# Loading k of two chunks at once, splitting the first-stage table, and rewriting VectorE's order in the first pass

## The chip, the cores and the metric

The kernel runs on one core of a Trainium2 chip. Its engines work side by side, each through its own queue in order: TensorE (PE, matmuls and transposes into PSUM; PEld is its weight load), VectorE (DVE), ScalarE (ACT), GpSimd (POOL) and SyncE (SP), which issues nearly all transfers (DMAs). Engines wait for one another by semaphores. The metric is device time in microseconds (us), lower is better: the median of 3 runs before is 234.06 (233.75 to 234.32).

## The reference

Two branches share one normalized input, and their results are added to it. Sequence length S is 2048, width D is 640, hidden width F is 1728; all tensors are bf16.

```
x  = A_q;  xn = (x - mean) / sqrt(var + 1e-5)          # per row, over D
# branch A: a shift convolution of 4 taps, a product, a long convolution
k_shift[s] = sum over t of k[s - t] * shift_k[:, t]    # t = 0..3, zero before the start
kv  = k_shift * v
y   = irfft(rfft(kv padded to 2S) * rfft(ssm_k padded to 2S))[:S]
y   = y + kv * ssm_D
A   = xn * y
# branch B: a gated unit
h   = sigmoid(xn @ w_gate) * (xn @ w_up)
B   = h @ w_down
out = x + A + B
```

## The kernel before

Rows are laid out 16 to a partition: row 16 p + b is on partition p, block b (b = 0..15). The 640 columns are 5 chunks c of 128.

**The gated unit** runs in four passes t, one per group of 4 blocks (512 rows). A pass needs the 4 blocks of xn transposed (xnT): in the first pass TensorE transposes them, in the others SyncE issues four transposing DMAs (xn_turn, L250). Then for each of 13 slices of 128 hidden columns come a gate product (gate_mm), its sigmoid on ScalarE (gate_ev), an up product (up_mm), and VectorE's product of the two into hT (up_ev, L286). A last slice, both_mm, holds the remaining 64 columns of both. Then the down products: for each block bb and each half of the columns, 7 + 7 matmuls (down_mm, part 0 and part 1, L315), after which VectorE adds the PSUM result to x (down_ev, L320). The PSUM pool of these products has 4 buffers, so a product waits until the fourth one before it has been read.

**Normalization** of groups 1 to 3: VectorE makes the statistics of 4 blocks (ln_norms, L200 and L204), GpSimd the factor (ln_pow, L212, once for the group), and VectorE normalizes (ln_xn, L217); for group 1, ScalarE does blocks 2 and 3 (ln_xn_act, L229), with a shift from GpSimd.

**The long convolution** is a Fourier transform in two stages, by chunk. For chunk c, VectorE makes kv in 16 steps (kv_op): per half of 8 blocks one product acc = k * tap 0 (L348), three products with later taps (L352), each added to acc (L354), and the product with v (L357). k lies in a tile kx with 3 extra rows ahead, the halo, from the partition before. There were two such tiles, one for even and one for odd chunks. The taps come by a broadcast load into sraw and are reordered into sc (taps: chunk 0 on GpSimd, others on ScalarE). The filter ssm_k is loaded to hn and transposed by VectorE in two steps (h_turn, L334) into the same tile kvh as kv; D is added to its first element on GpSimd (add_D, L328). Then stage one is eight steps per chunk (st1_mm: half h of the table and 4 blocks each, L374 and L376), copied out (st1_ev) and written to a buffer in DRAM (wr1). Stage two, the product in the frequency domain and the way back follow, through DRAM again.

**The order** of everything is written out by hand: each letter of the string ORDER takes the next step of one chain (m: first loads, g: products of the gated unit, u: VectorE's part of them, k: kv_op, H: h_turn, l: normalization, e: xn_turn, a and A: stage one and its copies, and so on). Each engine runs its instructions in that order. The tables and loads are issued by SyncE in the order of the list of chain m. Many transfers are under way at once; SyncE waits with an issue when the buffer it fills is still read, when an earlier transfer that shares its semaphore hasn't landed, or when the queue takes no more.

Of the kernel before, what the change touches and what calls it, by code (L numbers as in the profile page):

```python
# [34 lines left out]
def _tables():  # L35

    p = np.arange(P)  # L40
    k1 = p + 0.25
    s1 = np.zeros((P, NB, 2, P))
    for b in range(NB):
        psi = 2 * np.pi * k1[None, :] * (16 * p + b)[:, None] / 2048.0
        s1[:, b, 0, :] = np.cos(psi)
        s1[:, b, 1, :] = -np.sin(psi)
    tb = s1.transpose(3, 2, 1, 0) / 2048.0
# [10 lines left out]
def kernel(  # L58
# [14 lines left out]
    nc = tc.nc  # L73
# [24 lines left out]
    S1t = res.tile([P, NB, 2, P], U16, name="S1t")  # L98
    TBt = res.tile([P, 2, NB, P], U16, name="TBt")
    SMt = res.tile([P, 3, 32], U16, name="SMt")  # L100
    S1 = S1t.bitcast(BF16)
    TB = TBt.bitcast(BF16)
    SM = SMt.bitcast(BF16)
# [31 lines left out]
    def load_h(c):  # L135

        d = cin[c]
        d["hn"] = cv.tile([P, 4, 512], BF16, name="hn")
        d["dr"] = cv.tile([1, P], BF16, name="dr")
        sync.dma_start(d["dr"][:, :], Drow[:, c * P:(c + 1) * P])  # L140
        for q in range(4):
            src = A_ssm_k[c * P:(c + 1) * P, 512 * q:512 * q + 512].rearrange("(k r) t -> r k t", k=4)
            sync.dma_start(d["hn"][32 * q:32 * q + 32, :, :], src)

    def load_taps(c):
        cin[c]["sraw"] = cv.tile([P, 4 * P], BF16, name="sraw")
# [178 lines left out]

    def add_D(c):
        h0 = cin[c]["kvh"][0:1, 1, 0:2, :].rearrange("p b c -> p (b c)").rearrange("p (c e) -> p e c", e=2)[:, 0, :]
        nc.gpsimd.tensor_tensor(h0, h0, cin[c]["dr"][:, :], ALU.add)  # L328

    def h_turn(c, n):  # L330

# [34 lines left out]
    def st1_mm(c, n):  # L366

        h, n4 = divmod(n, 4)
        if n == 0:
            chunks[c]["d1"] = dr.tile([P, 2, NB, 2 * P], BF16, name="d1", bufs=2)  # L370
        pss[n] = ps = psC.tile([P, 4, 2 * P], F32, name="ps1", tag="c")
        for i in range(4):
            b = 4 * n4 + i
            nc.tensor.matmul(ps[:, i, 0:P], lhsT=S1[:, b, h, :], rhs=cin[c]["kvh"][:, 0, b, :], start=True, stop=True)  # L374
            hp = cin[c]["kvh"][:, 1, :, :].rearrange("p b c -> p (b c)").rearrange("p (b c e) -> p b e c", b=8, e=2)
            nc.tensor.matmul(ps[:, i, P:2 * P], lhsT=S1[:, b, h, :], rhs=hp[:, b // 2, b % 2, :], start=True, stop=True)  # L376

    def st1_ev(c, n, copy=act_copy):
        d = chunks[c]
# [19 lines left out]
    def rd2(s):  # L399

        c, s4 = divmod(s, 4)
        at = spare.get(s)
        if at is None:
            t2 = cv.tile([P, 8, 2 * P], BF16, name="t2", bufs=2)[:, :, :]
        else:
            t2 = (xn[:, 12:NB, :].rearrange("p b d -> p (b d)")[:, 0:2048] if at == 2 else
                  S1[:, 8 * at:8 * at + 8, :, :].rearrange("p b h k -> p (b h k)")).rearrange("p (r e) -> p r e", r=8)
# [43 lines left out]
    def inv1_ev(y, n, copy=act_copy):  # L451
        d = chunks[y // 2]
        if n == 0:
            d["ao", y] = kxs[1][:, 0:NB, :] if y >= 7 and y % 2 else cv.tile([P, 16, P], BF16, name="ao")[:, :, :]
# [14 lines left out]
    def rdb(c, n):  # L469

        d = chunks[c]
        if c >= 3 and n == 1:
            bi = kxs[0][:, 0:NB, :].rearrange("p (h b) c -> p h b c", h=2)
        elif c and n == 1:
            bi = S1[:, 8:NB, :, :].rearrange("p (h b) s c -> p h (b s) c", h=2)
        else:
            bi = cv.tile([P, 2, 8, P], BF16, name="bi")[:, :, :, :]
        src = d["d2"].rearrange("r (q h b) c -> (r q) h (b c)", q=NQ, h=2)
        sync.dma_start(bi.rearrange("p h b c -> p h (b c)"), src[:, :, 1024 * n:1024 * n + 1024])
        d["bi", n] = bi  # L480
# [8 lines left out]
                                 start=(h == 0), stop=(h == 1))  # L489

    def inv2_q(c, m):
        chunks[c]["yx", m] = yx = cv.tile([P, 4, P], BF16, name="yx")
# [58 lines left out]
    for t in range(4):  # L551
        for fc in range(0 if t else 2, 13):
            step("g", gate_mm, t, fc)
            step("s", gate_ev, t, fc)
            step("g", up_mm, t, fc)
            step("u", up_ev, t, fc)
        step("g", both_mm, t)
        step("s", both_ev, t)
        step("u", both_mul, t)
        firsts = [(0, 0, 0), (0, 1, 0), (0, 0, 1), (0, 1, 1)]  # L560
        for bb, e, part in firsts + [(k // 2, k % 2, n) for k in range(2, 8) for n in range(2)]:
            step("g", down_mm, t, bb, e, part)
            if part:
                step("u", down_ev, t, bb, e)
# [4 lines left out]
    def ks(c):  # L569
        return [(load_halo, c), (load_k, c, 0, 8), (load_k, c, 8, NB)]  # L570

    def vs(c):
        return [(load_v, c, 0, 8), (load_v, c, 8, NB)]

    for k in ((load_w, sync, 512, 1024, 0),
              (load_w, sync, 512, 1024, 1),
              (load_taps, 0),
              (sync.dma_start, SMt[:], SMd.ap()),
              (load_w, sync, 1024, 1280, 0),
              (load_w, sync, 1024, 1280, 1),  # L580
              (load_wd, sync, 0, 7),
              *ks(0),
              (load_w, sync, 1280, FF, 0),
              (load_w, sync, 1280, FF, 1),
              *hs(0),
              *vs(0),
              (load_wd, sync, 7, NFC),
              (sync.dma_start, S1t[:], S1d.ap()),
              *hs(1),
              (load_x, sync, 1),  # L590
              *ks(1),
              *vs(1)):
        step("m", *k)
    for k in ((load_x, sync, 2), (load_x, sync, 3), (sync.dma_start, TBt[:], TBd.ap())):
# [62 lines left out]
    step("o", store, NB - 1, NB, 4 * P, DM)  # L657

    ORDER = """
    mmggmmsgmuggmsgmgsuZumgggssumkgkguskugkkmsgugmmmmgkgmksgmuggHskkHkgsmukkgDumsgggkusumgTmkgkukagaumHg  # L660
    lllAKlgAatkwuAmmmakPPlAkgalAkkTwgaggagkegeugAxxDkkaeAaAgeKwaugkuAHkuggkAukkwsgkgkkgnustagukKKgghakA
    sulrwAsakggluglsaksAugHggkAVrubkkkBlswKBukgggaTVsgpkusukawgDkHPlngAaAaskgAKwAkukgskpbgtkBsllBugauAk
    gagpsAaguswVpakAguhkHHAgrgDkwcgVklguCkkraeCagAgkAbuBkuBkkggKgkbBKpggBaeualwukkggeIuurlTklAehrgwtVbBB
    ggagkAagppswuAagkuaKswrgpAAkaHAskWgHupDgakuVsAggswucglJukkgkrCsbgpBugaBaAgAWkkgsbspugPkrBgwpgsRnFku
    kgprcwgCJusgbgusgpuBdBWppbqrgsdBlRuqgBcqlCggJbsggksuBupgllkBbBgrqkWBgeaaeAAuppwdgaduRegaIAgrugpaAqae
    qggupAwcCqpJguugdbgFBgbBqqgugBppdcpWCuJqgrpsgqbgBsuwFgrgqsbuBgpBRsuWgpdcpqqdguJgqCsrrbFBgsgRbugBBpdr
    sppugcdCqugCqgbsgWBqpqggusrBRbpudgrgqWspBpBqcupdJsgCbgRBpgBqqguWgsppuqscCudgJsguqgqgRdWgoquuqoddRggg
    Rqquqguoqoggdoouqdgdqgqdqqqugoggqqugoooouooo
    """
    left = {k: iter(v) for k, v in chains.items()}  # L670
    for k in "".join(ORDER.split()):
# [33 lines left out]
```

## Time and profile before

| what | before |
|---|---|
| median of 3 runs | 234.06 us (233.75 to 234.32) |
| the profiled execution | 234.78 us, span 233.0 us |
| granted TensorE clock | 1.00 |
| moved by DMA | 56.79 MB, 244 GB/s over the span |
| SyncE's queue | 95702 packets, 92.6% of 16 engines' span |

The span is the time from the first to the last instruction. The page gives each engine's busy time, the chain of work that ended last (followed back from the end), and groups of equal instructions with their mean duration and the idle time before them. A line of the timeline has the start in us, the duration in us, engine, line, operation and tiles; in square brackets is the idle time of the engine before it and what ended that wait. A line of a window has the window, each engine's busy us with the number of instructions, TensorE's clock, the DMA share, and GB/s. Instructions on one engine overlap a little, so the spacing of their starts is less than their duration.

### The profile page before, as it was taken

How to read it: one execution, taken by the hardware profiler on the slowest of the kernel's cores; microseconds unless marked ns; L12 is line 12 of the kernel's file. 1: busy time of each engine (PE TensorE's matmuls, PEld its weight loads, DVE VectorE, ACT ScalarE, POOL GpSimd, SP SyncE). 2: the span in 40 equal slices, each digit the busy share in tenths (PEclk: the TensorE clock that was granted, in tenths of full speed). 3: DMA queues.
4: the chain of work that ended last, by engine and by line, in shares of the span. 5: the costliest groups of instructions: out<-in, count | busy, mean ns of one | idle time of the engine just before them, and what ended most of it. 6: DMA issues, size and time to landing. Idle time of an engine off the chain costs nothing.

```text
span 233.0 us, 5431 instructions
## 1 busy us (share of the span) xinstructions
PE 227.5 (98%) x2199; PEld 130.9 (56%) x2200; DVE 203.4 (87%) x357; ACT 123.5 (53%) x158; POOL 12.4 (5%) x26
## 2 busy tenths in 40 slices
PE   7999999997999999999999999999999999999995
PEld 2844446776454555677554544478654544446772
DVE  5444899799999999999999999997799999997773
ACT  2533321676364887765675847674556667752000
POOL 5210010040001100000011000000000000000000
PEclk9999999999999999999999999999999999999999
DMA  6999999896999969999989899689989999364884
GB/s 199 325 329 208 267 317 294 208 266 143 330 221 303 299 221 242 263 223 230 329 237 277 224 319 272 184 217 190 269 210 311 279 263 254 117 169 117 220 266 136
DMA packets 96159, 56.79 MB, mean 244 GB/s; under 512 B 55878, under 2 KB 90374, under 8 KB 95878
## 3 DMA queue, kind: packets, MB, share of 16 engines
q1 hardware_dynamic: 95702, 56.03, 92.6%
q10 hardware_dynamic: 432, 0.41, 0.5%
q8 instruction: 17, 0.28, 0.5%
q14 instruction: 8, 0.07, 0.1%
HBM read 36.12 MB, written 18.35 MB: 234 GB/s over the span
## 4 chain that ended last, share of the span: by engine, by line
PE 87%; DVE 5%; DMA 4%; issue 1%; SPq 1%; ACT 0%; DVEq 0%
PE pu L271 22%; PE pg L271 22%; PE pd L315 21%; PE psb L488 4%; DMA x<-in_A_q_dram 4%; PE ps L374 3%; PE ps L376 3%; PE ps L418 3%; PE psa L447 2%; PE idle L514 2%; PE pg L292 1%; DVE st L200 1%; PE pg L262 1%; PE pu L262 1%; DVE acc L354 1%
## 5 line engine op out<-in xcount | busy, mean ns | idle before, releaser
L271 PEld LDWEIGHTS <-w 128*128 128x128 bf16 x500 | 46.7, 98 | 53.9 <-issue 4.3
L315 PE MATMUL pd<-wd,hT 128*128 128x320 bf16 (+2 forms) x447 | 65.9, 299 | 0.1
L271 PE MATMUL pu<-xnT,w 128*128 128x512 bf16 x250 | 62.2, 379 | 0.0
L271 PE MATMUL pg<-xnT,w 128*128 128x512 bf16 x250 | 62.2, 379 | 0.0
L315 PEld LDWEIGHTS <-hT 128*128 128x128 bf16 x448 | 41.7, 98 | 18.2 <-issue 2.4
L280 ACT ACTIVATE sig<-pg 128x512 bf16<-128x512 f32 x52 | 31.1, 601 | 30.5 <-PE pg L271 23.8
L286 DVE TENSOR_TENSOR hT<-sig,pu 128x512 bf16<-128x512 bf16 x52 | 35.0, 682 | 10.8 <-PE pu L271 6.9
L232 ACT CAST xz<-ps 128x1024 bf16<-128x1024 f32 x36 | 35.1, 1014 | 15.5 <-PE ps L418 15.5
L232 ACT CAST t<-ps 128x1024 bf16<-128x1024 f32 x24 | 23.8, 1012 | 16.7 <-PE ps L376 14.5
L433 DVE TENSOR_TENSOR xz<-xz 128x2048 bf16<-128x2048 bf16 x20 | 24.4, 1221 | 0.2
L374 PE MATMUL ps<-kvh,S1t 128*128 128x128 bf16 x160 | 21.5, 218 | 1.2 <-DVE kvh L357 1.2
L376 PE MATMUL ps<-kvh,S1t 128*128 128x128 bf16 x160 | 21.6, 220 | 0.0
L354 DVE TENSOR_TENSOR acc<-acc,tmp 128x1024 bf16<-128x1024 bf16 x30 | 20.5, 684 | 0.3
L352 DVE TENSOR_TENSOR tmp<-kx,sc 128x1024 bf16<-128x1024 bf16 x30 | 20.5, 682 | 0.3
L320 DVE TENSOR_TENSOR x<-pd,x 128x320 bf16<-128x320 f32 (+2 forms) x32 | 15.2, 484 | 3.8 <-PE pd L315 3.6
L374 PEld LDWEIGHTS <-S1t 128*128 128x128 bf16 x160 | 15.5, 97 | 3.9 <-DVE kvh L357 1.4
L376 PEld LDWEIGHTS <-S1t 128*128 128x128 bf16 x160 | 15.4, 96 | 2.7 <-issue 0.2
L200 DVE BATCH_NORM_STATS2 st<-x 128x6 f32<-128x320 bf16 x32 | 13.8, 473 | 2.3 <-DMA x<-in_A_q_dram 2.3
L232 ACT CAST TBt<-ps 128x1024 bf16<-128x1024 f32 x14 | 13.8, 1012 | 2.7 <-PE ps L376 2.7
L493 DVE TENSOR_TENSOR yx<-psb,xn 128x512 bf16<-128x512 f32 x20 | 13.7, 687 | 1.4 <-PE psb L488 0.8
L431 DVE STREAM_SHUFFLE xz<-xz 128x512 f32<-128x512 f32 x20 | 14.6, 729 | 0.0
L232 ACT CAST ao<-psa 128x1024 bf16<-128x1024 f32 x9 | 9.0, 1013 | 8.6 <-PE psa L447 6.9
(56 smaller groups left out, 159.2 us busy)
## 6 DMA issues: line engine op xcount, KB each, us to landing
t<-d SPq DMA_DIRECT2D x15, 512.0 KB, 6.0
d<-t SPq DMA_DIRECT2D x13, 512.0 KB, 4.1
d<-TBt SPq DMA_DIRECT2D x7, 512.0 KB, 5.9
d<-ao SPq DMA_DIRECT2D x6, 512.0 KB, 5.5
bi<-d SPq DMA_DIRECT2D x6, 512.0 KB, 5.4
kx<-in_A_k_dram SPq DMA_DIRECT2D x10, 256.0 KB, 5.8
hn<-in_A_ssm_k_dram SPq DMA_DIRECT2D x20, 128.0 KB, 5.0
kvh<-in_A_v_dram SPq DMA_DIRECT2D x10, 256.0 KB, 5.2
```

Source lines behind the costliest of these rows:

```text
L200: nc.vector.bn_stats(st[:, i, SD * s2:SD * s2 + SD], x[:, b, s2 * 320:(s2 + 1) * 320])
L232: nc.scalar.copy(out=out, in_=in_)
L271: nc.tensor.matmul(pg[:, :], lhsT=w[:, c, u * UP + fc * P:u * UP + (fc + 1) * P], rhs=xnT[:, :, c, :], start=(c == 0), stop=(c == NC - 1))
L280: nc.scalar.activation(sig[fc][:, :], pgs[0, fc][:, :], ACT.Sigmoid)
L286: nc.vector.tensor_tensor(hT[:, fc, :], sig[fc][:, :], pgs[1, fc][:, :], ALU.mult)
L315: nc.tensor.matmul(pd[:, :], lhsT=hT[:, fc, bb * P:(bb + 1) * P], rhs=wd[:, fc, es], start=(fc == 0), stop=(fc == NFC - 1))
L320: nc.vector.tensor_tensor(x[:, 4 * t + bb, es], pds[bb, half][:, :], x[:, 4 * t + bb, es], ALU.add)
L352: nc.vector.tensor_tensor(d["tmp"][:, :, :], kx[:, lo + 3 - m:hi + 3 - m, :], sb(m), ALU.mult)
L354: nc.vector.tensor_tensor(d["acc"][:, :, :], d["acc"][:, :, :], d["tmp"][:, :, :], ALU.add)
L374: nc.tensor.matmul(ps[:, i, 0:P], lhsT=S1[:, b, h, :], rhs=cin[c]["kvh"][:, 0, b, :], start=True, stop=True)
L376: nc.tensor.matmul(ps[:, i, P:2 * P], lhsT=S1[:, b, h, :], rhs=hp[:, b // 2, b % 2, :], start=True, stop=True)
L433: nc.vector.tensor_tensor(z[:, 1:3, :, :], z[:, 0:1, :, :].to_broadcast((P, 2, 8, P)), z[:, 1:3, :, :], ALU.mult)
```

## The change

It has these parts, all in the first pass and ahead of it:

- k of chunks 0 and 1 gets one tile kx2 of [128, 19, 2, 128]: for each row block the 128 columns of chunk 0, then those of chunk 1. Two loads (blocks 0 to 7, 8 to 15) and two halo loads bring both chunks, in pieces of 256 columns (512 B) instead of 128. Chunks 2 to 4 are loaded one at a time into every other 128 columns of it, as before into kx0 and kx1.
- The first-stage table S1 is stored with its two halves outermost, and loaded in two transfers of 512 KB; x of group 1 is loaded between them. Places in the table that are reused later as buffers are renamed accordingly.
- D is loaded once, whole, instead of 128 elements per chunk.
- In the list of first loads, k, v of chunk 0, and the taps of chunk 1 come earlier, the first half of the down weights, wd, later.
- In pass 0 the down products of blocks 0 and 1 all do their first half ahead of any second half.
- VectorE's order: chunk 0's kv starts one eviction earlier, its h_turn come after it; chunk 1's kv steps 0 to 6 come ahead of the down evictions and the statistics of group 1, with the rest behind.
- sraw and yx share one buffer.

After the first 180 of the 839 steps (841 before) the order is the same as before.

```diff
-    s1 = np.zeros((P, NB, 2, P))
+    s1 = np.zeros((P, 2, NB, P))
...
-    kxs = [res.tile([P, NB + 3, P], BF16, name="kx%d" % i) for i in range(2)]
-    for kx in kxs:
-        nc.gpsimd.memset(kx[0:1, 0:3, :], 0.0)
+    kx2 = res.tile([P, NB + 3, 2, P], BF16, name="kx2")
+    kxs = [kx2[:, :, i, :] for i in range(2)]
+    kxf = kx2.rearrange("p r e c -> p (r e c)")
+    nc.gpsimd.memset(kx2[0:1, 0:3, :, :], 0.0)
...
+        if c == 0:
+            sync.dma_start(Dt[:, :], Drow[:, :])
-        d["dr"] = cv.tile([1, P], BF16, name="dr")
-        sync.dma_start(d["dr"][:, :], Drow[:, c * P:(c + 1) * P])
...
+    def load_k2(lo, hi):
+        sync.dma_start(kx2[:, lo + 3:hi + 3, :, :].rearrange("p b c e -> p b (c e)"), kr[:, lo:hi, 0:2 * P])
+
+    def load_halo2():
+        for lo, hi in ((16, P), (1, 16)):
+            sync.dma_start(kx2[lo:hi, 0:3, :, :].rearrange("p b c e -> p b (c e)"),
+                           kr[lo - 1:hi - 1, NB - 3:NB, 0:2 * P])
...
-            nc.tensor.matmul(ps[:, i, 0:P], lhsT=S1[:, b, h, :], rhs=cin[c]["kvh"][:, 0, b, :], start=True, stop=True)
+            nc.tensor.matmul(ps[:, i, 0:P], lhsT=S1[:, h, b, :], rhs=cin[c]["kvh"][:, 0, b, :], start=True, stop=True)
...
-        firsts = [(0, 0, 0), (0, 1, 0), (0, 0, 1), (0, 1, 1)]
+        firsts = [(k // 2, k % 2, n) for n in range(2) for k in range(2 if t else 4)]
...
               (sync.dma_start, SMt[:], SMd.ap()),
+              (load_halo2,),
+              (load_k2, 0, 8),
+              (load_k2, 8, NB),
+              (load_v, 0, 0, 8),
               (load_w, sync, 1024, 1280, 0),
               (load_w, sync, 1024, 1280, 1),
-              (load_wd, sync, 0, 7),
-              *ks(0),
+              (load_v, 0, 8, NB),
               (load_w, sync, 1280, FF, 0),
               (load_w, sync, 1280, FF, 1),
               *hs(0),
-              *vs(0),
+              (load_wd, sync, 0, 7),
               (load_wd, sync, 7, NFC),
-              (sync.dma_start, S1t[:], S1d.ap()),
+              (sync.dma_start, S1t[:, 0, :, :], S1d.ap()[:, 0, :, :]),
+              (load_x, sync, 1),
+              (sync.dma_start, S1t[:, 1, :, :], S1d.ap()[:, 1, :, :]),
               *hs(1),
-              (load_x, sync, 1),
-              *ks(1),
               *vs(1)):
```

The head of ORDER as VectorE sees it, up to where both orders agree again:

```
before: up_ev(0,2) ... up_ev(0,5) kv(0,0) kv(0,1) up_ev(0,6) kv(0,2) up_ev(0,7) kv(0,3) kv(0,4)
        up_ev(0,8) kv(0,5) kv(0,6) up_ev(0,9) h_turn(0,0) kv(0,7) kv(0,8) h_turn(0,1) kv(0,9)
        up_ev(0,10) kv(0,10) kv(0,11) up_ev(0,11) kv(0,12) up_ev(0,12) both_mul kv(0,13) kv(0,14)
        down_ev(0,0,0) kv(0,15) down_ev(0,0,1) h_turn(1,0) ln_norms(1,0..3) kv(1,0) down_ev(0,1,0)
        kv(1,1) ln_xn(1,0) kv(1,2) ln_xn(1,1) kv(1,3..5) down_ev(0,1,1) kv(1,6) kv(1,7)
        down_ev(0,2,0) kv(1,8) down_ev(0,2,1) h_turn(1,1) kv(1,9) down_ev(0,3,0) kv(1,10)
        down_ev(0,3,1) kv(1,11..15)
after:  up_ev(0,2) ... up_ev(0,4) kv(0,0) kv(0,1) up_ev(0,5) kv(0,2) kv(0,3) up_ev(0,6) kv(0,4)
        kv(0,5) up_ev(0,7) kv(0,6..8) up_ev(0,8) kv(0,9) kv(0,10) up_ev(0,9) kv(0,11..13)
        up_ev(0,10) kv(0,14) kv(0,15) up_ev(0,11) h_turn(0,0) up_ev(0,12) h_turn(0,1) both_mul
        kv(1,0..6) down_ev(0,0,0) down_ev(0,0,1) ln_norms(1,0) down_ev(0,1,0) ln_norms(1,1)
        down_ev(0,1,1) ln_norms(1,2) ln_norms(1,3) h_turn(1,0) ln_xn(1,0) ln_xn(1,1) kv(1,7..10)
        down_ev(0,2,0) kv(1,11) down_ev(0,2,1) kv(1,12) h_turn(1,1) down_ev(0,3,0) kv(1,13)
        down_ev(0,3,1) kv(1,14) kv(1,15)
```

TensorE's order in the same stretch, after: four down products of part 0 (blocks 0 and 1), then part 1 of (0,0,0), st1(0,0), part 1 of (0,0,1), st1(0,1), part 1 of (0,1,0), st1(0,2), st1(0,3), part 1 of (0,1,1), and from st1(0,4) on as before.

More of the change, by code (lines that the diff above doesn't have):

```diff
@@ L41, in _tables @@
     k1 = p + 0.25
-    s1 = np.zeros((P, NB, 2, P))
+    s1 = np.zeros((P, 2, NB, P))
     for b in range(NB):
         psi = 2 * np.pi * k1[None, :] * (16 * p + b)[:, None] / 2048.0
-        s1[:, b, 0, :] = np.cos(psi)
-        s1[:, b, 1, :] = -np.sin(psi)
-    tb = s1.transpose(3, 2, 1, 0) / 2048.0
+        s1[:, 0, b, :] = np.cos(psi)
+        s1[:, 1, b, :] = -np.sin(psi)
+    tb = s1.transpose(3, 1, 2, 0) / 2048.0
     th = 2 * np.pi * np.outer(np.arange(NB), np.arange(NB)) / 16.0
@@ L97 @@
     nc.gpsimd.memset(mhalf[:], -0.5)
-    S1t = res.tile([P, NB, 2, P], U16, name="S1t")
+    S1t = res.tile([P, 2, NB, P], U16, name="S1t")
     TBt = res.tile([P, 2, NB, P], U16, name="TBt")
     SMt = res.tile([P, 3, 32], U16, name="SMt")
+    Dt = res.tile([1, DM], BF16, name="Dt")
     S1 = S1t.bitcast(BF16)
@@ L145, in load_taps @@
     def load_taps(c):
-        cin[c]["sraw"] = cv.tile([P, 4 * P], BF16, name="sraw")
+        cin[c]["sraw"] = cv.tile([P, 4 * P], BF16, name="sraw", tag="sy")
         sync.dma_start(cin[c]["sraw"][:], srow[:, 4 * c * P:4 * (c + 1) * P].to_broadcast((P, 4 * P)))
@@ L373, in st1_mm @@
             b = 4 * n4 + i
-            nc.tensor.matmul(ps[:, i, 0:P], lhsT=S1[:, b, h, :], rhs=cin[c]["kvh"][:, 0, b, :], start=True, stop=True)
+            nc.tensor.matmul(ps[:, i, 0:P], lhsT=S1[:, h, b, :], rhs=cin[c]["kvh"][:, 0, b, :], start=True, stop=True)
             hp = cin[c]["kvh"][:, 1, :, :].rearrange("p b c -> p (b c)").rearrange("p (b c e) -> p b e c", b=8, e=2)
-            nc.tensor.matmul(ps[:, i, P:2 * P], lhsT=S1[:, b, h, :], rhs=hp[:, b // 2, b % 2, :], start=True, stop=True)
+            nc.tensor.matmul(ps[:, i, P:2 * P], lhsT=S1[:, h, b, :], rhs=hp[:, b // 2, b % 2, :], start=True, stop=True)
     def st1_ev(c, n, copy=act_copy):
@@ L453, in inv1_ev @@
         if n == 0:
-            d["ao", y] = kxs[1][:, 0:NB, :] if y >= 7 and y % 2 else cv.tile([P, 16, P], BF16, name="ao")[:, :, :]
+            d["ao", y] = kxf[:, 2048:4096].rearrange("p (b c) -> p b c", c=P) if y >= 7 and y % 2 else cv.tile([P, 16, P], BF16, name="ao")[:, :, :]
         dst = d["ao", y].rearrange("p (s g e) c -> p g s (e c)", s=2, g=4)
@@ L491, in inv2_q @@
     def inv2_q(c, m):
-        chunks[c]["yx", m] = yx = cv.tile([P, 4, P], BF16, name="yx")
+        chunks[c]["yx", m] = yx = cv.tile([P, 4, P], BF16, name="yx", tag="sy")
         nc.vector.tensor_tensor(yx[:, :, :], chunks[c]["pb", m][:, :, :], xn[:, 4 * m:4 * m + 4, c * P:(c + 1) * P],
@@ L559 @@
         step("u", both_mul, t)
-        firsts = [(0, 0, 0), (0, 1, 0), (0, 0, 1), (0, 1, 1)]
-        for bb, e, part in firsts + [(k // 2, k % 2, n) for k in range(2, 8) for n in range(2)]:
+        firsts = [(k // 2, k % 2, n) for n in range(2) for k in range(2 if t else 4)]
+        for bb, e, part in firsts + [(k // 2, k % 2, n) for k in range(len(firsts) // 2, 8) for n in range(2)]:
             step("g", down_mm, t, bb, e, part)
@@ L659 @@
     ORDER = """
[L660 to L668, printed above, removed]
+    mmmZmmmmmmmmmTmmmmmmmggsguggsggsuukkgggssukkggukksukkkgsgukkgggsgukkkggsgsukkguHstggguHDmmmsukkkkkkk
+    ggguaguaAKgluaAwAaAglullPPHDalAlkTwgakkggakgegegAxxaeAaAgeKwaukgukAHukggAukkwsgggnustagukKKgghakAsul
+    rwAsakggluglsaksAugHggkAVrubkkkBlswKBukgggaTVsgpkusukawgDkHPlngAaAaskgAKwAkukgskpbgtkBsllBugauAkgagp
+    sAaguswVpakAguhkHHAgrgDkwcgVklguCkkraeCagAgkAbuBkuBkkggKgkbBKpggBaeualwukkggeIuurlTklAehrgwtVbBBggag
+    kAagppswuAagkuaKswrgpAAkaHAskWgHupDgakuVsAggswucglJukkgkrCsbgpBugaBaAgAWkkgsbspugPkrBgwpgsRnFkukgprc
+    wgCJusgbgusgpuBdBWppbqrgsdBlRuqgBcqlCggJbsggksuBupgllkBbBgrqkWBgeaaeAAuppwdgaduRegaIAgrugpaAqaeqggup
+    AwcCqpJguugdbgFBgbBqqgugBppdcpWCuJqgrpsgqbgBsuwFgrgqsbuBgpBRsuWgpdcpqqdguJgqCsrrbFBgsgRbugBBpdrsppug
+    cdCqugCqgbsgWBqpqggusrBRbpudgrgqWspBpBqcupdJsgCbgRBpgBqqguWgsppuqscCudgJsguqgqgRdWgoquuqoddRgggRqquq
+    guoqoggdoouqdgdqgqdqqqugoggqqugoooouooo
     """
```

8 lines of the change are left out of this document (4 added, 4 removed).

## The prediction

> **What bounds the kernel now.** I read the page's busy shares first, then the chain that ended last, the list of waits, and the timelines of TensorE, VectorE, GpSimd and SyncE from 25 to 64 us. Busy shares:
> ```profile
> PE 227.5 (98%) x2199; PEld 130.9 (56%) x2200; DVE 203.4 (87%) x357; ACT 123.5 (53%) x158; POOL 12.4 (5%) x26
> ```
> TensorE sets the time: 98% of the span. VectorE is second; from 28 us on it has hardly a gap. So an edit is worth what it takes out of TensorE's gaps. TensorE's timeline shows one after the start-up:
> ```profile
> 53.82 0.22 PE L376 MATMUL ps<-kvh,S1t 128*128 128x128 bf16 x1
> 55.24 0.23 PE L374 MATMUL ps<-kvh,S1t 128*128 128x128 bf16 x1 [1.20 <-DVE kvh L357]
> ...
> 58.06 1.24 PE L271 MATMUL pg<-xnT,w 128*128 128x512 bf16 x5
> ```
> Neighbouring matmuls of this kind start 0.06 apart, so from 53.82 to 55.24 about 1.36 us are lost: stage one of chunk 1 waits for its kv product. The last line is the second pass's first gate product. In the chain, the stretch before the gap leaves TensorE and runs back through VectorE to a load:
> ```profile
> 35.46 8.80 DMA x<-in_A_q_dram
> 44.29 0.90 DVE st L200 x2
> ...
> 54.49 0.70 DVE kvh L357
> 55.24 0.23 PE ps L374
> ```
> x of group 1 lands at 44.27, VectorE takes its statistics, then makes chunk 1's kv, and TensorE waits. That load was issued late because SyncE first waited to reuse D's buffer:
> ```profile
> SPq L140 <- POOL kvh L328: 1.6, 1, 1.6
> SPq L143 <- DVE kvh L334: 1.2, 1, 1.2
> ```
> **The most that can be won** is this 1.36 us, plus a 0.14 us gap at 46.09 (a matmul waits for a PSUM copy behind the taps copy on ScalarE): 1.5 us, if nothing new waits.
>
> **Part 1: VectorE's new order.** I lay VectorE's queue out again with spacings from its own timeline:
> ```profile
> 59.49 0.69 DVE L352 TENSOR_TENSOR tmp<-kx,sc 128x1024 bf16<-128x1024 bf16 x1
> 60.22 0.69 DVE L354 TENSOR_TENSOR acc<-acc,tmp 128x1024 bf16<-128x1024 bf16 x1
> 60.94 0.69 DVE L352 TENSOR_TENSOR tmp<-kx,sc 128x1024 bf16<-128x1024 bf16 x1
> ```
> Start to start: 0.72 us where an operation needs the one before, 0.60 where it doesn't; 1.02 for a transpose, 0.40 for a down eviction, 0.99 for one block's statistics. Chunk 0's kv now starts when up_ev(0,4) is done (18.73 + 0.61 = 19.34, before 22.14) and uses the idle time between evictions; the queue falls behind only at up_ev(0,8) (27.8 against 27.36). It has caught up at up_ev(0,12), 36.0, which TensorE sets. From there: h_turn(0,1) 36.6, both_mul 37.7, seven steps of chunk 1's kv from 38.4 (0.60 + 5 x 0.72 + 0.60) to 43.2, two down evictions to 44.0, statistics 0 to 45.0, eviction, statistics 1 from 45.4 to 46.4, then down_ev(0,1,1).
>
> TensorE there: the down products start at 36.80 as before. The order is now four first halves, then second halves with stage one between. With 0.95 us for 7 matmuls and 0.45 for a stage-one step: (0,0,0,1) ends at 41.56, (0,0,1,1) 42.97, (0,1,0,1) 44.38, (0,1,1,1) 46.24. Its eviction can start at 46.4, so VectorE and TensorE meet here. Statistics 2 and 3 then run from 46.84 to 48.84. Before, they were through at 48.34 (where the next operation starts). So chunk 1's kv is early and **the statistics of group 1 end 0.5 us later**, although x comes earlier.
>
> TensorE without a new wait: the later order is as before, less the gap and the 0.14: stage one of chunk 1 at 53.77, first gate product of pass two at 56.58 instead of 58.06. Chunk 1's first kv half is then ready: ln_xn(1,1) at 50.75, kv_op(1,7) at 51.2 to 51.9; its h half at 49.9 and D on GpSimd by 51.8. The old gap goes, with 1.9 us to spare.
>
> **Part 2: what is late next.** The gate product needs four transposed blocks of xn. Their chain before:
> ```profile
> 48.56 1.28 POOL L212 TENSOR_TENSOR rstd<-mv,mhalf 128x4 f32<-128x4 f32 x1 [16.49 <-DVE mv L204]
> ...
> 50.39 5.25 SPq L250 DMA_TRANSPOSE xnT<-xn x4
> ```
> The four issues take 1.3 us each whatever else goes on; the fourth starts at 54.41, and with the 2.6 us that the shortest of this group took to land it is in at 57.0, 1.0 us before 58.06. This margin is all that the chain leaves. It now starts 0.5 us later: ln_xn(1,0) at 50.4 instead of 49.89, transposes from 50.9, landed at 57.55, gate product at 57.6. TensorE arrives at 56.58 and waits 1.0 us. **Gain: 58.06 - 57.6 = 0.46 us.** From both sides: nothing (58.06) if the chain starts another 0.46 later; 1.48 if the chain were 1.0 us faster than worked out, for which I see no row, since evictions bound by TensorE hold it. I take 0.46.
>
> Queued behind these waits: on SyncE the transposes hold load_k(2), two wr1 and x of group 2, which shift by 0.5 at most; ScalarE's ln_xn_act ends at 52.5 and st1_ev(0,6) at 53.5, just ahead of the stage-one step at 53.77 that needs its PSUM buffer (0.2 to spare). VectorE ends chunk 1's kv at about 59.8 instead of 63.1, against stage-one step (1,2) at 62.9: 3 us to spare where it had 0.4.
>
> **Part 3: the loads.** k of two chunks goes ahead of the last gate and up weights, with v of chunk 0, and the first half of the down weights behind. Rates by window:
> ```profile
> 5.00:8.00 3.00, 2.87 (x34) 1.92 (x33) 3.00 (x10) 1.27 (x4) 1.11 (x2) 1.00 1.14 312
> 18.50:19.80 1.30, 1.30 (x8) 0.59 (x7) 0.69 (x1) 0.06 (x1) 0.00 (x0) 1.00 1.35 226
> 28.30:30.00 1.70, 1.70 (x10) 0.78 (x8) 1.52 (x3) 0.60 (x1) 0.00 (x0) 1.00 1.34 209
> 22.90:26.30 3.40, 3.40 (x18) 1.53 (x16) 2.83 (x5) 0.69 (x2) 0.00 (x0) 1.00 1.15 327
> 30.40:44.30 13.90, 13.90 (x96) 8.54 (x95) 12.16 (x19) 4.41 (x6) 0.78 (x1) 1.00 1.01 284
> ```
> The last column is GB/s: weights in pieces of 512 B and more 312 to 327, k in 256 B 226, v in 256 B 209, the mixed stretch 284. Ahead of the last up weights: down weights gone, 1.147 MB at 327: -3.5 us; k as 1.049 MB at 312 instead of 0.524 at 226: +1.0; wider halo +0.3; v +2.5; taps +0.4. Sum +0.7: they land at 27.0 instead of 26.3 and are needed at 30.33. Then at 284 (v at 209): h 29.2, down weights 33.2 and 36.9 (needed 36.8 and 40.6), table half one 38.8 (41.6), x 41.1 (44.0), half two 42.9 (46.2), h of chunk 1 44.8 (48.8), v 47.3 (51.2). All hidden, with 2.8 us or more. Bounds: down to 200 GB/s for k (+1.9 us) the loads stay hidden; nothing is won by an earlier one.
>
> The row for pieces of 512 B and up implies 1.45 times as long for 512 B as for 256 B. The Trainium skill, page DMA: Bandwidth & Descriptors, section Why small descriptors are slow (HBM only), counts 32 B beats and about 3 cycles a packet, so 11 cycles for 256 B; my estimate from it is 19 for 512 B, 1.73 times. By it k would take 4.0 us instead of 3.4 and x would land at 41.7: hidden too, and a little more weight for the late load below.
>
> **Part 4: the rest.** kv reads kx in runs of 128 elements, 512 B apart. Cost 0, by the nearest row with runs of 128 in a wider tile:
> ```profile
> L352 DVE TENSOR_TENSOR tmp<-kx,sc 128x1024 bf16<-128x1024 bf16 x30 | 20.5, 682 | 0.3
> L498 DVE TENSOR_TENSOR x<-x,yx 128x512 bf16<-128x512 bf16 x20 | 8.4, 422 | 0.3
> ```
> Half the elements in 0.62 of the time: no loss by strides (a dense tile has a fixed part too). Upper bound: one element a cycle, as the 1024-element copies from PSUM on VectorE, 1212 ns: +0.53 per read. D once: four issues of 0.25 to 0.45 less on SyncE, and its 1.6 us wait goes. Taps of chunk 1 move on ScalarE ahead of both_ev: 0.66 us in a gap of 1.5. One wider memset on GpSimd: 0.4 to 0.8, before a 1.3 us gap. The reuse of kx, table and sraw/yx space falls after the last readers in the unchanged part of the order. All 0.
>
> **Sum against the profiled execution:** 234.78 us, span 233.0 (1.78 around it); span after 232.5. The median of the runs, 234.06, is 0.72 below the profiled time; I take the 0.46 from it: **233.6**.
>
> **Rivals.** *A, no new wait*: the transposes come as early as TensorE, 234.06 - 1.48 = 232.6. For it: x is there 3 us earlier. Against: two of four statistics stand behind an eviction that TensorE releases at 46.4. *B, the gap only moves*: VectorE 0.3 to 0.6 us slower than laid out (each of 20 operations 20 to 30 ns more), gate product near 58.0: 234.0. *C, slower by a late load*: x of group 1 now stands behind both down weights and half the table. If it lands after 44.0, the statistics, and with them the transposes, slip by the same; from 44.5 on the kernel is slower. In 20 to 22 us the queue moved only 119 GB/s; two such breaks (2.5 us) plus a landing like that of the table, 10.1 us after issue, put it at 45.3: gate product at 58.9, 234.9. Against it: 2.9 us of margin. *D, strides halve VectorE's rate*: the change is then worth +0.53 on 12 reads ahead of the statistics, less 1 us of idle time, over 5 us: 239 or more. The row at 422 ns speaks against it. The Trainium skill, page VectorE: DVE Perf Modes, Rules for kernel authors, asks for "dense step-1" for double rate; read strictly that is D, and the trace bears it out only for the step, not for dense rows.
>
> **Chances.** My forecast 0.53 (its own range 233.3 to 233.9, so about evenly on both sides of the 0.47 us, 0.2%, that a measurement here can tell: 0.30 faster, 0.23 same); A 0.12, faster; B 0.11 (0.09 same, 0.02 slower); C 0.19, slower; D 0.05, slower. Faster 0.42, same 0.32, slower 0.26. Range: 232.7 (into A) to 234.9 (C's price), leaving out about half of A, D and C's tail.
>
> **What would show it.** In TensorE's timeline: no gap ahead of stage one of chunk 1, but one of about 1 us ahead of the first gate product of pass two, near 57.6, released by the transposes. On VectorE: first kv near 19.3, last statistics of group 1 near 48.8. kv reads at 0.68 us. x landed by 42. Wrong it would be if that gate product came at 56.6 (A) or after 58.1 (B, C), if L352 took over 0.75 us (D), or if a weight load released a matmul before 36.8.

## The result, and the profile after

| | before | after |
|---|---|---|
| median (range, runs) | 233.93 us (233.52 to 235.11, 21) | 234.97 us (234.65 to 237.52, 21) |
| ratio after to before | | 1.0053, 95% interval 1.0037 to 1.0069 |
| profiled execution, span | 234.78 us, 233.0 us | 234.76 us, 232.9 us |

The changed kernel is 0.5% slower, about 1.0 to 1.2 us, where 0.5 us faster was forecast. The two profiled executions, though, take the same time. That contradiction is the point of this case. (The medians and ranges here count every run; the ratios leave disturbed runs out.)

The busy shares of the page after have hardly moved:

```profile
PE 227.5 (98%) x2200; PEld 130.7 (56%) x2200; DVE 203.7 (87%) x357; ACT 123.3 (53%) x158; POOL 12.2 (5%) x25
```

TensorE's timeline after, around the end of the first pass (start, duration, engine, line, operation, tiles; in brackets the idle time before and what ended it):

```profile
54.03 0.22 PE L384 MATMUL ps<-kvh,S1t 128*128 128x128 bf16 x1
...
58.08 1.24 PE L281 MATMUL pg<-xnT,w 128*128 128x512 bf16 x5 [1.08 <-DMA xnT<-xn]
```

The matmul at 54.03 is the first of chunk 1's stage one: it follows its neighbour by 0.06 us, and the old gap of 1.36 us is gone. The last line has a new one: the first gate product of pass two waits 1.08 us for the transposed xn.

VectorE's timeline after, and then SyncE's queue, the chain that leads to that wait:

```profile
43.71 0.89 DVE L330 TENSOR_TENSOR x<-pd,x 128x320 bf16<-128x320 f32 x2
44.51 0.88 DVE L210 BATCH_NORM_STATS2 st<-x 128x6 f32<-128x320 bf16 x2
45.43 0.22 DVE L214 BATCH_NORM_AGGREGATE mv<-st 128x2 f32<-128x15 f32 x1
45.57 0.43 DVE L330 TENSOR_TENSOR x<-pd,x 128x320 bf16<-128x320 f32 x1
...
49.21 0.22 DVE L214 BATCH_NORM_AGGREGATE mv<-st 128x2 f32<-128x15 f32 x1
49.39 1.11 DVE L344 STREAM_TRANSPOSE kvh<-hn 128x512 f32<-128x512 f32 x1
50.63 0.80 DVE L227 TENSOR_SCALAR xn<-x,mv,rstd 128x640 bf16<-128x640 bf16 x2
```
```profile
51.14 5.27 SPq L260 DMA_TRANSPOSE xnT<-xn  x4
```

The first block's statistics start at 44.51 with no wait: VectorE is busy with chunk 1's kv and the evictions until then, and x had landed at 41.91. The last are through at 49.39, where the next operation starts. In VectorE's timeline before, the last is this line, and the next operation starts at 48.34:

```profile
48.20 0.22 DVE L204 BATCH_NORM_AGGREGATE mv<-st 128x2 f32<-128x15 f32 x1
```

So the four transposes are issued from 51.14 (before 50.39), and the last lands at 57.83.

A measure that is free of the start-up is the time from TensorE's first down product of pass 0 to the first gate product of pass two. In three profiled executions in which TensorE doesn't wait in between (of three kernels shown further down) it is 19.74 us; what an execution has above that is counted as lost there. TensorE's timeline has the first down product in these lines, before and then after:

```profile
36.80 3.97 PE L315 MATMUL pd<-wd,hT 128*128 128x320 bf16 x28
```
```profile
37.10 4.92 PE L325 MATMUL pd<-wd,hT 128*128 128x320 bf16 x35
```

| profiled execution | first down product | first gate product of pass two | lost, us |
|---|---|---|---|
| before | 36.80 | 58.06 | 1.52 |
| after | 37.10 | 58.08 | 1.24 |

### The profile page after: what moved, and what is told of

Same layout as the page of the kernel before. It is cut to its first block, busy times and chain, and to the rows that moved or that the text cites. A ratio compares the mean times of both kernels' runs of the same rounds, so it can differ in the third digit from the quotient of the medians.

```text
span 232.9 us, 5418 instructions
## 1 busy us (share of the span) xinstructions
PE 227.5 (98%) x2200; PEld 130.7 (56%) x2200; DVE 203.7 (87%) x357; ACT 123.3 (53%) x158; POOL 12.2 (5%) x25
## 4 chain that ended last, share of the span: by engine, by line
PE 94%; DMA 4%; SPq 1%; issue 0%; ACT 0%; DVE 0%
PE pd L325 26%; PE pu L281 24%; PE pg L281 24%; PE psb L498 4%; PE ps L386 4%; PE ps L384 4%; PE ps L428 3%; PE psa L457 2%; DMA w<-in_B_w_up_dram 2%; PE pg L302 2%; DMA xnT<-xn 1%; PE pu L272 1%; PE pg L272 1%; PE pt L252 0%; ACT TBt L242 0%
## 5 line engine op out<-in xcount | busy, mean ns | idle before, releaser
L325 PEld LDWEIGHTS <-hT 128*128 128x128 bf16 x448 | 41.7, 98 | 18.2 <-issue 2.4
```

The costliest lines, as they stand in the source:

```text
L325: nc.tensor.matmul(pd[:, :], lhsT=hT[:, fc, bb * P:(bb + 1) * P], rhs=wd[:, fc, es], start=(fc == 0), stop=(fc == NFC - 1))
```

## The experiments

Each batch ran on one chip, with runs of the kernel before beside it. Before's medians there were 234.09, 234.08, 234.04 and 234.01 us.

**First batch.** Theory 1 of the expectations is that the wait has moved from chunk 1's kv to the transposes, held by VectorE's statistics, and that ordinary runs of before lose less at their gap than its profiled execution shows. Its rival puts the loss on other things: the gap as large as profiled, or the loads.

*Before, a second profile.* No edit.

> The kernel before, unchanged, profiled once more. Theory 1 (the wait only moved): the profiled execution of before lay 0.85 us above the median of its runs, so it is no typical one; a second profile has a gap ahead of stage one of chunk 1 of 0.4 to 0.7 us instead of 1.36, and a span near 232.2. Rival (the profile is typical and the change loses elsewhere): the gap is 1.2 to 1.5 us again.

Measured: 234.48 us, span 232.6. The gap is there again in TensorE's timeline, 0.88 us idle (1.06 us lost by the measure above, 36.91 to 57.71):

```profile
54.89 0.23 PE L374 MATMUL ps<-kvh,S1t 128*128 128x128 bf16 x1 [0.88 <-DVE kvh L357]
```

It lies between both expectations and decides nothing. Both profiled executions (234.78, 234.48) lie above the median of 234.09, but not outside the ordinary runs: of the 113 runs of before in this record 19 took 234.48 us or more, and 12 took 234.78 or more.

*After, a second profile.* No edit.

> The changed kernel, unchanged, profiled once more. Theory 1: a gap of 1.1 us ahead of the first gate product of pass two again (58.08 in the first profile, released by the fourth transpose). Theory 2 (the start-up): the last up product of the start is held by its weights as in the first profile, and pass 0's down products start 0.3 us later than before's 36.80; if the start is only scatter between executions, they start at 36.8 here or also shift in the second profile of before.

Measured: 237.24 us, span 235.4. In this execution loads are late, one after the other, as TensorE's timeline shows:

```profile
38.30 4.93 PE L325 MATMUL pd<-wd,hT 128*128 128x320 bf16 x35 [0.95 <-DMA wd<-in_B_w_down_dram]
...
43.43 0.23 PE L384 MATMUL ps<-kvh,S1t 128*128 128x128 bf16 x1 [0.20 <-DMA S1t<-tabS]
...
48.54 0.23 PE L384 MATMUL ps<-kvh,S1t 128*128 128x128 bf16 x1 [0.27 <-DMA S1t<-tabS]
...
60.53 1.24 PE L281 MATMUL pg<-xnT,w 128*128 128x512 bf16 x5 [1.49 <-DMA xnT<-xn]
```

The second half of the down weights landed at 41.69 instead of 38.73, x of group 1 at 45.96 instead of 41.91, from an identical program. So late loads are a second cost, in part of the executions. The wait for the transposes is there again, longer. For the start this execution tells little, since its down products wait for weights; in before's second profile they start at 36.91.

*Statistics ahead of kv.* The changed kernel with another order on VectorE: only five kv steps of chunk 1 ahead, then one block's statistics ahead of each down eviction.

```diff
- kv(1,0..6) down_ev(0,0,0) down_ev(0,0,1) ln_norms(1,0) down_ev(0,1,0) ln_norms(1,1) down_ev(0,1,1)
- ln_norms(1,2) ln_norms(1,3) h_turn(1,0) ln_xn(1,0) ln_xn(1,1) kv(1,7..10)
+ kv(1,0..4) ln_norms(1,0) down_ev(0,0,0) ln_norms(1,1) down_ev(0,0,1) ln_norms(1,2) down_ev(0,1,0)
+ ln_norms(1,3) down_ev(0,1,1) h_turn(1,0) ln_xn(1,0) ln_xn(1,1) kv(1,5..10)
```

> The changed kernel with VectorE's order alone edited: after five of chunk 1's kv steps the statistics of group 1 run, one ahead of each down eviction, and kv steps 5 to 7 follow the normalization. Theory 1: statistics end near 47.5 instead of 49.4, the transposes are in near 56.2 and TensorE arrives at 56.8 without a gap: 1.0 to 1.2 us faster than the changed kernel, about 233.8, ratio to before 0.998 to 1.000. Theory 2 (the loss is in the start and in the loads): the gap goes but the time stays within 0.4 us of the changed kernel, ratio 1.004 to 1.006.

Measured: 236.39 us median (234.93 to 238.55, 6 runs), ratio 1.0116 (1.0068 to 1.0164): slower, not faster. VectorE's timeline in its profile:

```profile
44.05 0.89 DVE L210 BATCH_NORM_STATS2 st<-x 128x6 f32<-128x320 bf16 x2 [1.25 <-DMA x<-in_A_q_dram]
```

VectorE was free for the statistics at 42.8, and waited 1.25 us for x, which landed at 44.03. By the measure above this execution loses 0.88 us (37.67 to 58.29), 0.36 less than the changed kernel's profile, but its down products start 0.57 later. The new order alone wins nothing in the times; in this execution because x isn't there to be used. What the runs of 237 us and more wait for, no profile shows.

**Second batch.** Theory V: the usual loss of the changed kernel is VectorE's place for the statistics. Theory L: it is loads that land late in a saturated queue.

*After, timed again.* No edit.

> The changed kernel, unaltered, as the measure for the next two on the same chip. From the 21 runs so far: median near 235.0 us, most within 234.7 to 235.3, and one in five or six above 235.5. Theory V (the time is set by when the transposes of xn land, which VectorE's statistics set) explains the narrow part; theory L (loads arrive too late in a saturated queue) explains the upper runs, and perhaps the whole.

Measured: 235.2 us (234.9 to 239.46, 12 runs), ratio 1.0074 (1.0045 to 1.0103); seven of 12 within 234.9 to 235.21, five above 235.9. The profiled execution has the same wait, and loses 1.23 us by the measure above (37.54 to 58.51).

*Without the second half of the down weights.* That load goes; GpSimd fills its place with zeros, so the kernel leaves out half of the down products' sum.

```diff
-              (load_wd, sync, 7, NFC),
+              (nc.gpsimd.memset, wd[:, 7:13, :], 0.0),
+              (nc.gpsimd.memset, wd[64:P, 13, :], 0.0),
```

> The changed kernel without the load of the second half of the down weights (rows 896 to 1727 are zero, filled by GpSimd; so the down products leave out half of their sum). This takes 1.04 MB, some 3.7 us at 284 GB/s, out of the queue ahead of the table and x of group 1. Theory V: x is not what holds VectorE in the typical run, so the wait of about 1.1 us ahead of the first gate product of pass two stays and the median stays at 234.7 to 235.0; only the runs above 235.5 go. Theory L: the median falls by 1 us or so to 233.9 or less, and the wait with it.

Measured: 234.89 us (234.65 to 236.93, 12 runs), ratio 1.0042 (1.0022 to 1.0063). Eleven runs lie within 234.65 to 235.14. The upper runs are nearly gone, and the body is where it was. In the profile x lands at 40.54, nothing waits for it, and the wait stays in TensorE's timeline (0.97 us lost by the measure above, 37.53 to 58.24):

```profile
58.24 1.25 PE L281 MATMUL pg<-xnT,w 128*128 128x512 bf16 x5 [0.80 <-DMA xnT<-xn]
```

*The same, with the statistics ahead.* Both edits together.

> The same omission, with VectorE's order of the earlier run with the statistics ahead: five kv steps of chunk 1, then one block's statistics ahead of each down eviction, the rest of kv behind. In that run x had landed too late for it to help. If the end of the wait is x and then the statistics (V and L together), both are now early: the wait ahead of the gate product goes below 0.4 us, and the time falls below no_wd2 by 0.7 to 1.1 us, to about 233.6 to 234.0. If the time stays with no_wd2, neither x nor the statistics set the transposes, but something in SyncE's queue does.

Measured: 233.85 us (233.72 to 235.18, 12 runs), ratio 0.9989 (0.9969 to 1.0009), 1.04 us below the kernel without that load, from VectorE's order alone, as its expectation had it. VectorE's timeline, first and last statistics, and then TensorE's:

```profile
42.33 0.89 DVE L210 BATCH_NORM_STATS2 st<-x 128x6 f32<-128x320 bf16 x2
...
47.60 0.22 DVE L214 BATCH_NORM_AGGREGATE mv<-st 128x2 f32<-128x15 f32 x1
```
```profile
57.05 1.25 PE L281 MATMUL pg<-xnT,w 128*128 128x512 bf16 x5
```

Statistics end 1.6 us earlier than in the changed kernel, and the gate product has no wait. So V holds for the usual loss, L for the upper runs, and neither edit alone brings back the time of before. x landed at 42.30 here, about as in two of the three profiles of the changed kernel (41.91 and 42.38): leaving the load out may spare the late landings more than it moves the usual one, but single profiles can't show that.

*Before, with x early.* Before, plus three pieces: D once, the table in two halves with x between, the four statistics of group 1 ahead of h_turn(1,0).

```diff
-              (sync.dma_start, S1t[:], S1d.ap()),
-              *hs(1),
+              (sync.dma_start, S1t[:, 0, :, :], S1d.ap()[:, 0, :, :]),
               (load_x, sync, 1),
+              (sync.dma_start, S1t[:, 1, :, :], S1d.ap()[:, 1, :, :]),
+              *hs(1),
```

> The kernel before with three pieces: D loaded once, the table in two halves with x of group 1 between, and the four statistics of group 1 ahead of the first transpose of h of chunk 1. No k of two chunks, no new order of kv, down products as before. Theory L and V agree here: x lands near 41 instead of 44.3, the statistics end near 46 instead of 48.3, kv of chunk 1 is done by about 53, the gap of 1.36 us ahead of its stage one closes to under 0.3, the transposes have 2 us to spare: 0.5 to 1.2 us faster than before, 232.9 to 233.6. Rival: before's unprofiled runs lose little at that gap (their median is 0.4 to 0.7 us below the profiled runs), so that only 0 to 0.4 us is won.

Measured: 234.04 us (233.54 to 234.56, 12 runs), ratio 0.9996 (0.9981 to 1.001): no change. Yet in its profile x landed at 39.24 and the gap is gone; the first gate product starts 19.74 us after the first down product, at 56.95 with no wait (TensorE's timeline):

```profile
56.95 1.24 PE L272 MATMUL pg<-xnT,w 128*128 128x512 bf16 x5
```

The 1.1 to 1.5 us that before's profiles show are gone from this one, and the ordinary time doesn't move. The rival on record is borne out.

**Third batch.** Theory P: before's gap belongs largely to its profiled executions, and ordinary runs have slack at this place. Rival G: it is lost in every run. Two kernels make VectorE later at just that place, by making chunk 1's first kv product more than once.

```diff
-            nc.vector.tensor_tensor(d["acc"][:, :, :], kx[:, lo + 3:hi + 3, :], sb(0), ALU.mult)
+            for _ in range(2 if c == 1 and half == 0 else 1):
+                nc.vector.tensor_tensor(d["acc"][:, :, :], kx[:, lo + 3:hi + 3, :], sb(0), ALU.mult)
```

> The kernel before with one more VectorE operation, chunk 1's first kv product made twice, right behind the statistics of group 1: 0.6 us more ahead of chunk 1's stage one. Theory P (the gap of 1.1 to 1.4 us ahead of that stage is hardly there in ordinary runs; it belongs to the profiled executions): there is slack, so less than 0.3 us slower, and its profile shows a gap of 1.7 to 2.0. Rival G (the gap is there in every run): 0.6 us slower, 234.7.

Measured: 234.97 us (234.19 to 237.44, 12 runs), ratio 1.0043 (1.0017 to 1.0069), that is 0.4 to 1.6 us. P's "less than 0.3" falls, and G's 234.7 is within the interval: there is no slack at this place. The profiled execution lost 2.11 us there, and more behind it, shown under the hardware below. TensorE's timeline:

```profile
56.26 0.23 PE L375 MATMUL ps<-kvh,S1t 128*128 128x128 bf16 x1 [1.96 <-DVE kvh L358]
```

With the product four times in place of twice (range(4)):

> The same with the product made four times, 1.8 us more. Theory P: slower by 1.8 us less the slack, 0.8 to 1.6 us, and less than the profile's own gap grows. Rival G: 1.8 us slower, 235.9.

Measured: 236.07 us (235.19 to 238.2, 6 runs), ratio 1.0099 (1.0061 to 1.0138). That is 1.4 to 3.2 us slower. G's 235.9 lies in it, and P's 0.8 to 1.6 only with its upper end. But what is added counts in full wherever there is no slack, whether before itself loses 1.4 us there or nothing, so the two kernels don't decide how much before loses. TensorE's timeline tells something of that:

```profile
55.87 0.23 PE L375 MATMUL ps<-kvh,S1t 128*128 128x128 bf16 x1 [1.66 <-DVE kvh L358]
```

By the measure above it loses 1.83 us with 1.8 us of added work: by this count before itself would have lost nothing in such an execution. There the statistics started at 42.89 without waiting for x, where in before they waited until 44.29. So the gap comes and goes with the landing of x.

*The changed kernel with k of chunk 1 late.* k of the two chunks is loaded apart (chunk 1's behind the table), and chunk 1's kv follows the statistics, as before; all else of the change stays.

```diff
-              (load_halo2,),
-              (load_k2, 0, 8),
-              (load_k2, 8, NB),
+              *ks(0),
...
+              *ks(1)[:2],
               *hs(1),
+              *ks(1)[2:],
               *vs(1)):
```

> The changed kernel with k of the two chunks loaded apart again (chunk 0 where the change has it, chunk 1 behind the table), and chunk 1's kv steps 0 to 6 behind the statistics of group 1, as before; chunk 0's new order, the split table with x between, D once, and the order of the down products stay. If the loss comes from chunk 1's kv ahead of the statistics and from k of chunk 1 ahead of the other loads, all of it goes: no wait above 0.3 us ahead of stage one of chunk 1 or of the first gate product of pass two, 233.8 to 234.2 us, and none of 12 runs above 235.5. If another part costs, part of the loss stays: 234.5 or more.

Measured: 234.52 us (233.69 to 236.43, 12 runs), ratio 1.0032 (1.0011 to 1.0054). In the profile (233.86 us) the up weights land at 27.00 (28.82 in the changed kernel), x at 39.88, and TensorE waits nowhere between 9 and 64 us; its timeline has

```profile
57.04 1.24 PE L281 MATMUL pg<-xnT,w 128*128 128x512 bf16 x5
```

The expectation is half met: an execution without any wait exists, six of 12 runs lie within 233.69 to 234.35, but three lie above 235.5, and the median is the one named for the case that another part costs. Part of the loss stays that this profile doesn't show; which wait makes it is open.

**Fourth batch.** *Before, without the second half of the down weights*: the same edit as above, on before.

> The kernel before without the load of the second half of the down weights (those rows are zero, filled by GpSimd; half of the down products' sum is left out): 1.04 MB, 3.7 us at 284 GB/s, less ahead of x of group 1 and h of chunk 1, nothing else changed. The gap ahead of stage one of chunk 1 must go from its profile. What its ordinary runs win is what before's ordinary runs lose there: theory P now says 0.3 to 0.5 us (233.5 to 233.8); rival G, that the profiled 1.1 to 1.4 us are lost in every run, says 232.7 to 233.0.

Measured: 233.81 us (233.39 to 234.55, 12 runs), ratio 0.9993 (0.998 to 1.0006). The gap is gone from its profile, as TensorE's timeline shows (37.02 to 56.76, 19.74 us), and ordinary runs win 0.16 us, 0.47 at most by the interval of the ratio:

```profile
37.02 3.97 PE L315 MATMUL pd<-wd,hT 128*128 128x320 bf16 x28
...
56.76 1.24 PE L271 MATMUL pg<-xnT,w 128*128 128x512 bf16 x5
```

Rival G, which said 232.7 to 233.0, falls: **the usual run of before loses 0 to 0.5 us at the gap, where its two profiled executions lost 1.06 and 1.52.** These two are like the slowest sixth of its ordinary runs; whether profiling makes the gap likelier is open.

*The changed kernel with the statistics ahead, and x ahead of the second half of the down weights.*

```diff
+              (load_x, sync, 1),
               (load_wd, sync, 7, NFC),
               (sync.dma_start, S1t[:, 0, :, :], S1d.ap()[:, 0, :, :]),
-              (load_x, sync, 1),
```

> The changed kernel with the statistics ahead on VectorE, as in the earlier run, and with x of group 1 loaded ahead of the second half of the down weights. Theory L+V: in this queue one load can come earlier only if another comes later. x lands near 39 and the transposes no longer hold TensorE, but that half of the weights lands 2.3 us later, at 40.5 to 41.5, where the second halves of the down products ask for it at about 41, and the table halves land near 42 and 44.5: TensorE waits at one of these by 0 to 1.5 us, 233.9 in the best runs and 234.5 or more in the median. Rival: there is room for it, and the median is 233.8 to 234.0, no slower than before.

Measured: 235.86 us (233.8 to 239.33, 12 runs), ratio 1.0056 (1.0032 to 1.008). One run of 12 reaches 233.8; the median doesn't. The profiled execution (238.91 us) is one of the three longest of the 12, so its waits are not those of a usual run; TensorE's timeline shows what it waits for:

```profile
42.82 1.11 PE L325 MATMUL pd<-wd,hT 128*128 128x320 bf16 x7 [1.15 <-DMA wd<-in_B_w_down_dram]
45.78 0.29 PE L384 MATMUL ps<-kvh,S1t 128*128 128x128 bf16 x1 [1.84 <-DMA S1t<-tabS]
```

x lands at 39.62, and in turn the weights (42.78) and the table's first half (45.73) are late. Together with a lower clock behind them (shown under the hardware below) the waits make up its 4.86 us lost by the measure above. In this execution the one load came earlier at the cost of others, as expected, with larger waits than were named; for the median that is argued, not shown. None of these kernels is clearly faster than the kernel before: where its profile shows no gap at all the gain is about 0.2 us, and the interval includes none.

## Why the prediction was wrong

**The step that failed is the base of the sum**: "The median of the runs, 234.06, is 0.72 below the profiled time; I take the 0.46 from it." The 0.46 was the difference of two waits, the old gap of 1.5 us less a new wait of 1.0. The new wait is in the ordinary runs too: taking it away by VectorE's order was worth 1.04 us in medians. The old gap is not: taking it away in two other ways was worth 0.1 us (x early, ratio 0.9996) and 0.16 us (a load left out, ratio 0.9993), and both intervals include nothing. So a gain that ordinary runs don't have was set against a loss that they do have. With before's ordinary loss in place of its profiled one the same sum reads -0.2 + 1.24 = about +1.0 us, and +1.0 is what the medians show. That the two agree so closely is in part luck: before's loss is known only to within 0 to 0.5 us, and the later start after the change (below) is not in the sum. The warning stood in the table: the profiled execution was 0.72 us above the median of the runs, which is half of the gap that it shows.

- *The view that bounds the kernel.* Right that TensorE's gap ahead of stage one of chunk 1 is the only large one, and that x is behind it. Wrong as the measure of what can be won.
- *Part 1, VectorE's order.* Right in kind: kv of chunk 1 is early (no gap at 54.03), the evictions meet TensorE, and the statistics of group 1 end later. First kv 19.63 (laid out 19.34), last statistics 49.39 (48.84). Of the 0.55 us some 0.3 come from TensorE's start (first down product 37.10 instead of 36.80), the rest from 1.05 us a block where 0.99 was taken.
- *Part 2, what is late next.* Right: the transposes, and a wait of 1.0 us, measured 1.08 and 1.06 in the two executions without late loads. Right for these executions that the four issues take about 1.3 us each, but not "whatever else goes on": with k of chunk 1 late the first of them took 2.2 us (49.19 to 51.41). The times were off by 0.2 to 0.5: issue from 51.14 (50.9), landed 57.83 (57.55), gate product 58.08 (57.6). In the profiled pair this ate the whole 0.46.
- *Part 3, the loads.* "All hidden, with 2.8 us or more" was too sure. Up weights landed at 28.82 instead of 27.0, x at 41.91 instead of 41.1, the halves of the down weights at 35.01 and 38.73 instead of 33.2 and 36.9, the second half of the table at 44.47 instead of 42.9: 0.8 to 1.8 us late even here, and up to 5.6 us late in the execution of 237.24 us (second half of the table at 48.49). The windows gave mean rates of one execution; the scatter between executions was not in them. For k of chunk 1 with the wider halo the sum had 1.0 + 0.3 us; without it ahead, up weights and x land 1.8 and 2.0 us earlier in the one profile of that kernel, so it may have been too small, but that difference is within the scatter. One term can be read directly: from 15 to 17 us of the changed kernel's profile nearly all packets were pieces of 512 B, most of them k, and the rate was 293 GB/s, not the 312 that was taken (0.2 us of the 1.8).
- *The Trainium skill's packet rule* (page DMA: Bandwidth & Descriptors, section Why small descriptors are slow (HBM only)), from which the prediction estimated 41.7 for x instead of 41.1: x landed at 41.91, nearer to that estimate, but the neighbouring loads were late too, so this landing doesn't separate the rule from them. The rate does a little: 293 GB/s against the 226 for pieces of 256 B is 1.54 times as long for a piece of 512 B, between the row's 1.45 and the estimate's 1.73.
- *Part 4.* Right on strides, so rival D falls: the reads of k take what they took, 683 ns against 682 (groups of instructions of the page after: count, busy us, mean ns, idle us before):

```profile
L362 DVE TENSOR_TENSOR tmp<-kx,sc 128x1024 bf16<-128x1024 bf16 x30 | 20.5, 683 | 0.3
```

  D once did take SyncE's wait for D away, but the load of h of chunk 1 then waited 5.8 us for the buffer that the later h_turn(0,1) frees, and landed at 47.13 instead of 44.8; its reader came at 49.39, so it cost nothing.
- *Rivals.* A didn't come: its condition, statistics free of the evictions, holds only with another order and an earlier x. B describes the profiled pair (gate product 58.08 against 58.06). C exists as forecast in kind, in part of the executions, and costs more than the 0.9 us given to it when weights and table are late as well.

The later start is a term that the prediction had at nothing ("the down products start at 36.80 as before"). The first down product comes at 37.10 to 37.69 in seven executions with the changed load order and 36.80 to 37.21 in six with the old one (the execution of 237.24 us, where it waited for weights, left out). This goes with up weights (columns 0 to 255) that land at 7.69 to 8.27 us instead of 7.21 to 7.62, though every weight load issued up to there is the same. Its cause stays open, and so does its price: the two kernels without that half of the down weights and without a wait, one with each load order, have medians of 233.85 and 233.81 us, so ordinary runs show next to nothing of it, though the intervals of their ratios leave room for some tenths of a us. The remaining scatter of the kernel with k of chunk 1 late is open too.

## What to carry to other kernels

Before a gap is counted as winnable, compare the profiled execution's time with the median of the ordinary runs: where it lies above by a good part of the gap, the profile may show one of the slower executions, and a cheap kernel that removes its cause (here one load left out) prices it before the order is rewritten. A chain that ends in a long serial tail, here four transposes of 1.3 us each, should get the engine's first free slot; work that is merely needed next can fill in behind it. In a queue as full as this one, moving a load forward can move others back, and margins have to be counted with the scatter of landings over several executions, not with one execution's mean rate.

## What was unexpected of the hardware

- *A wait of 2 us at TensorE was followed by half the clock, and cost the execution nearly twice its length.* In before with one added product, TensorE idled 1.96 us, and its clock was then granted at half for 3.4 us. The windows of that execution (window; busy us and instructions of PE, PEld, DVE, ACT, POOL; clock; DMA share; GB/s):

```profile
54.20:56.20 2.00, 0.10 (x2) 0.00 (x0) 1.97 (x5) 1.01 (x1) 0.00 (x0) 1.00 0.74 150
56.40:59.80 3.40, 3.40 (x24) 2.56 (x23) 3.40 (x7) 1.01 (x1) 0.00 (x0) 0.50 0.80 217
59.80:62.00 2.20, 2.20 (x14) 1.23 (x13) 1.47 (x3) 1.01 (x1) 0.00 (x0) 0.99 1.14 336
```

  The down products there start 0.267 us apart instead of 0.136. From first down product to gate product this execution lost 4.0 us: 2.1 of waiting and 1.9 of clock. In the execution of 238.91 us the clock fell likewise behind its two waits of 1.15 and 1.84 us (same columns):

```profile
46.50:49.00 2.50, 2.50 (x16) 1.70 (x15) 0.28 (x1) 1.01 (x1) 0.00 (x0) 0.51 1.24 154
```

  With waits of 1.66 us (three added products) and 1.08 us (the changed kernel) the clock stayed at 1.00. The Trainium skill, page TensorE: Matmul & The Clock Gate, section Why this matters for your kernels, asks for no idle gaps over about 3 us; here the clock fell after one of 1.96 us.
- *The landing of one load scatters by 4 us between executions of one program*: x of group 1 at 41.91, 42.38 and 45.96 us in three executions of the changed kernel.
